# Gate and up of three row groups by seven block products for eight, statistics on ScalarE, and x added by accumulating transfers

## The chip, the cores and the metric

The kernel runs on one core of one Trainium2 chip. The metric is the device time of one execution in microseconds (us). The core has five engines that follow their own instruction lists and wait for one another through semaphores: TensorE (PE, matrix products, with PEld for its weight loads), VectorE (DVE), ScalarE (ACT), GpSimd (POOL) and SyncE (SP, which here issues transfers).

## The reference, cut to what matters

```python
xn = _layernorm(x, axis=-1)                       # x: 2048 rows of 512, float32
s = irfft2(rfft2(xn) * (w_r + 1j * w_i))          # over rows and columns
gate, up = xn @ W_gate, xn @ W_up                 # 512 -> 1376 each
g = silu((relu(gate) * up) @ W_down)              # 1376 -> 512
return x + s * g
```

## The kernel before

**Precision.** Each float32 operand of a product is split into two float16 halves, high and low, and a product is three matmuls (`PASSES`: high by high, high by low, low by high) that accumulate in float32 in PSUM. So each operand costs two extra instructions wherever it is made: a cast to the high half, on ScalarE, and a subtraction that leaves the low half, on VectorE.

**The spectral path** (left factor `s`). The rows come in eight loads of 256 (`load_x`, 0 to 7). `stats` and `deviation`/`deviations` give the layer norm, `normalise` writes `xf`, `fold` makes the sums and differences of mirrored columns (`eo`, `ee`, `xs`), `split` the halves, and `first_stage` is the first transform along the rows (`s1`, tile `t`, to the scratch `A_d` in HBM). Eight `fft_chunk` calls follow: `y_stage`, `x_stage`, the multiplication by the filter (tiles `tt`, `po`, `pf`), `z_stage`, `v_stage`, and the scratch `C_d`. `last_stage`, eight times, reads `C_d` (tile `ct`), does the last transform (`s2`), scales it on ScalarE (`zz`) and unfolds the columns (`ae`, `ye`, `sv`).

**The gated path** (right factor `g`). The rows are four groups of 512 (index `c` or `k`). The 1376 hidden columns are ten blocks of 128 and a last one of 96 (`TAIL`). `product(c, f, i)` multiplies one group by one block of the gate (i = 0) or up (i = 1) weights: 12 matmuls of 512 columns, four of the inner dimension by three passes. The rows enter transposed, as tile `xT`; `turn` makes it for groups 1 to 3 by a DMA transposition, `turn_row` for group 0 on PE. `rectify` (ScalarE) and `hidden` (VectorE, ScalarE) evaluate relu(gate)·up and its two halves, tile `h16`; `down` multiplies by the down weights (tile `dn`), `gate` applies silu, tile `g`.

**The end.** `finish(c, i)` loads a 128-row block of x again (`xt`), multiplies `sv` by `g`, adds x, and stores. The last block of group 3 is done in two halves of columns (`columns`), the second in tile `dn_3b`.

**The order.** Nothing above runs in the order of the text. Every `step` gives an engine, an estimated cost, the names that it reads and writes, and perhaps a due time; `Plan.run` places all steps on the five engines by those estimates, the due times and the number of buffers in each pool, and then emits each engine's instructions in that order. The table of numbers at the top of the file (`T0`, `LOADS`, `LOADX`, `FIRST`, `MID`, `LAST`, ...) sets the due times. PSUM is three pools of two buffers here: `gu` for gate and up, `dn` for down, and `F` for the transforms (`gu` holds one bank each, `F` two).

The first work of PE is `keep_busy`, 78 matmuls on a constant (tile `idle`), until the first weights and rows are there. InOrder.__getattr__ wraps every engine call, so the profile gives one line (L64) to nearly every instruction; rows are told apart by the tiles' names.

```python
def product(c, f, i, rows=slice(0, 4), tag="gu"):
    ...
            for k in range(4):
                for h, l in PASSES:
                    w = wgt[:, k, 2 * h, :] if f == TAIL else wgu[g][:, h, i, k, o:o + P]
                    matmul(t[:, rows], w, xT[:, rows, l * 4 + k, :], start=n == 0, stop=n == 11)
```

## Time and profile before

| | |
|---|---|
| median of 3 runs | 411.29 us (411.02 to 412.25) |
| the profiled execution | 410.83 us, of which its span, first to last instruction, is 409.1 us |
| PE busy | 402.5 us of the span |
| DVE busy | 306.6 us |
| ACT busy | 190.0 us |
| POOL busy | 47.6 us |
| moved by DMA | 51.72 MB |
| granted PE clock | 0.997 of full speed |

How to read it: "busy" is the time in which an engine executes, and an engine that is not busy waits for a name that another engine or a transfer writes. A row such as `t<-s,t 128x896 f16<-128x896 f32 x2` says: two instructions that write tile `t` from tiles `s` and `t`, 128 partitions by 896 elements. An engine runs its instructions in the order of its list, so a wait holds up all that stands behind it.

### The profile page before, as it was taken

To read this page: it belongs to the slowest core of one execution; us is meant where nothing else is said; L and a number is where in the kernel's file an instruction comes from. 1 tells how busy PE (TensorE), PEld (TensorE's weight loads), DVE (VectorE), ACT (ScalarE), POOL (GpSimd) and SP (SyncE) were. 2 spreads that over 40 slices of the span, in tenths; PEclk is the share of its full clock that TensorE was granted. 3 is DMA by queue.
4 is the path that set the end of the run, shared out by engine and by line. 5 is a ranking of instruction groups with operands and counts; after the bars stand their busy time and mean duration, and the time that the engine had idled before them with its cause. 6 is when DMAs were issued, how large, how long until landed. Compare 5 with 4: busy or idle time off the path is not lost.

```text
span 409.1 us, 7662 instructions
## 1 busy us (share of the span) xinstructions
PE 402.5 (98%) x3023; PEld 213.4 (52%) x3023; DVE 306.6 (75%) x646; ACT 190.0 (46%) x359; POOL 47.6 (12%) x68
## 2 busy tenths in 40 slices
PE   8899999999999999999999999999999999999995
PEld 7784444544444444545465455556455445444554
DVE  3959999999999993515776977878863325999973
ACT  5999655435452549320445434536432327223321
POOL 0000000000000000001230312311311006133320
PEclk9999999999999999999999999999999999999998
DMA  8970210317138269753005144142322089656511
GB/s 285 416 253 6 98 49 3 92 64 154 44 111 145 59 182 355 209 170 116 2 0 168 34 135 125 58 155 57 115 51 53 0 192 221 210 177 211 176 53 52
DMA packets 34948, 51.72 MB, mean 126 GB/s; under 512 B 15392, under 2 KB 17024, under 8 KB 34912
## 3 DMA queue, kind: packets, MB, share of 16 engines
q1 hardware_dynamic: 34624, 50.71, 41.4%
q10 hardware_dynamic: 288, 0.52, 0.5%
q8 instruction: 23, 0.38, 0.4%
q14 instruction: 13, 0.11, 0.1%
HBM read 35.48 MB, written 12.60 MB: 118 GB/s over the span
## 4 chain that ended last, share of the span: by engine, by line
PE 98%; DVE 0%; ACT 0%; issue 0%
PE gu L64 55%; PE dn L64 27%; PE s L64 3%; PE z L64 3%; PE xx L64 3%; PE idle L64 2%; PE y L64 2%; PE v L64 2%; PE dn_3b L64 1%; PE head L64 0%; ACT xT L64 0%; PE sum L64 0%; DVE xT L64 0%; ACT g L64 0%; DVE sv L64 0%
## 5 line engine op out<-in xcount | busy, mean ns | idle before, releaser
L64 PE MATMUL gu<-xT,wgu 128*128 128x512 f16 (+1 forms) x1032 | 214.8, 364 | 1.2 <-ACT xT L64 1.0
L64 PEld LDWEIGHTS <-wgu 128*128 128x128 f16 x1032 | 99.4, 98 | 105.0 <-issue 4.6
L64 PE MATMUL dn<-wds,h 128*128 128x512 f16 (+2 forms) x528 | 115.5, 373 | 0.0
L64 PEld LDWEIGHTS <-h 128*128 128x128 f16 (+1 forms) x561 | 53.7, 98 | 57.7 <-issue 1.8
L64 DVE TENSOR_TENSOR h<-gu,r 128x512 f32<-128x512 f32 (+2 forms) x52 | 33.6, 646 | 26.4 <-PE gu L64 24.5
L64 ACT ACTIVATE h<-h 128x512 f16<-128x512 f32 (+1 forms) x44 | 27.4, 626 | 52.4 <-DVE h L64 50.6
L64 POOL TENSOR_TENSOR po<-tt,tt 128x256 f32<-128x256 f32 x16 | 14.8, 924 | 282.3 <-DVE tt L64 243.2
L64 ACT ACTIVATE r<-gu 128x512 f32<-128x512 f32 (+1 forms) x44 | 26.1, 593 | 30.3 <-PE gu L64 30.0
L64 DVE TENSOR_TENSOR h<-h,h 128x512 f16<-128x512 f32 (+1 forms) x44 | 29.9, 696 | 6.9 <-ACT h L64 6.8
L64 POOL TENSOR_TENSOR ae<-zz 128x128 f32<-128x128 f32 (+1 forms) x32 | 21.3, 698 | 62.5 <-ACT zz L64 43.2
L64 DVE SCALAR_TENSOR_TENSOR tt<-xsp,cw,wt 128x512 f32<-128x512 f32 x32 | 25.6, 863 | 0.0
L64 ACT ACTIVATE g<-dn,cdi 128x512 f32<-128x512 f32 (+1 forms) x16 | 10.3, 673 | 25.9 <-PE dn L64 25.8
L64 DVE TENSOR_TENSOR z<-z,z 128x1024 f16<-128x1024 f32 x8 | 9.8, 1222 | 14.1 <-ACT z L64 14.1
L64 DVE TENSOR_TENSOR sv<-sv,g 128x512 f32<-128x512 f32 (+1 forms) x17 | 11.8, 722 | 7.5 <-ACT g L64 6.9
L64 PE MATMUL gu<-xT,wgt 128*64 128x256 f16 (+1 forms) x144 | 16.9, 309 | 0.0
L64 DVE SCALAR_TENSOR_TENSOR wgu<-raw,p,wgu 128x512 f16<-128x512 f32 x20 | 14.3, 746 | 0.3 <-ACT wgu L64 0.3
L64 ACT ACTIVATE wgu<-raw 128x512 f16<-128x512 f32 x20 | 12.3, 619 | 4.0 <-DMA raw<-in_w 4.0
L64 DVE BATCH_NORM_STATS2 st<-x 128x6 f32<-128x512 f32 x16 | 10.8, 676 | 4.4 <-DMA x<-in_x 4.4
L64 ACT ACTIVATE xs<-xs 128x1024 f16<-128x1024 f32 x8 | 8.4, 1054 | 11.7 <-DVE xs L64 11.7
L64 PEld LDWEIGHTS <-wgt 128*64 128x64 f16 (+1 forms) x144 | 9.6, 106 | 7.4 <-issue 1.7
L64 DVE TENSOR_TENSOR xt<-xt,sv 128x512 f32<-128x512 f32 (+1 forms) x17 | 11.6, 710 | 2.5 <-DMA xt<-in_x 2.3
L64 DVE TENSOR_TENSOR a<-y,a 128x1024 f16<-128x1024 f32 x8 | 9.7, 1217 | 4.9 <-ACT a L64 4.9
(135 smaller groups left out, 431.8 us busy)
## 6 DMA issues: line engine op xcount, KB each, us to landing
A_d<-t SPq DMA_DIRECT2D x16, 256.0 KB, 3.3
rw<-in_wl SPq DMA_DIRECT2D x8, 512.0 KB, 8.7
wt<-in_wl SPq DMA_DIRECT2D x8, 512.0 KB, 4.9
at<-A_d SPq DMA_DIRECT2D x8, 512.0 KB, 5.3
C_d<-t SPq DMA_DIRECT2D x16, 256.0 KB, 3.3
ct<-C_d SPq DMA_DIRECT2D x16, 256.0 KB, 5.9
xt<-in_x SPq DMA_DIRECT2D x16, 256.0 KB, 3.0
out<-xt SPq DMA_DIRECT2D x15, 256.0 KB, 2.1
```

Source lines behind the costliest of these rows:

```text
L64: return lambda *args, **kw: self.tc.keep_in_program_order(f(*args, **kw))
```

## The change

- **Gate and up of groups 1 to 3 by Strassen's scheme.** For a pair of hidden blocks (`FAST`, five pairs; the last block stays as it was) the rows of a group are cut in two halves, the inner dimension in two halves, and gate and up are the two column blocks. Seven block products (p = 1 to 7, `fast_product`) take the place of eight. One product is 12 matmuls of 256 columns: two hidden blocks by two of the inner dimension by three passes. They accumulate in three PSUM tiles, `faa`, `fab` and `fad`, that are copied out and added as they grow (`fast_rest`): per pair and group three copies and two casts on ScalarE, and on VectorE three tensor additions or subtractions and four combined operations.
- **The operands of those products.** `weight_sums` loads the raw gate and up weights of each block again (`again`), scales them on ScalarE, forms four sums and differences (`t_0` to `t_9`), and splits them into `wt` and over the first half of the up weights in `wgu`. `prepare` reads the normalised rows back from a new scratch `X_d` (written by `keep_x`), splits and transposes them to `xT` as `turn` did, and does the same with four sums and differences of row halves, tiles `sf`, `s`, `S`.
- **Statistics of loads 2 to 7 on ScalarE** (two passes with an accumulated output for each block), and `normalise` there too.
- **The filter's products** in `fft_chunk`: the filter is scaled by `cw` on ScalarE first, and two VectorE instructions of 1024 elements take the place of four of 512; `common` is two instructions for four.
- **The unfolding of `ae`** goes from POOL to VectorE.
- **x is added by transfers.** Four DMAs copy x into the output early; `finish` multiplies `sv` by `g` and stores it with an accumulating DMA that POOL issues. The last block keeps the addition. `g` of groups 0 to 2 is put in a scratch `G_d` and read back.
- **Pools and numbers.** `gu` and `dn` become one pool `w` of four; `k4` has 10 buffers for 12, `k2` 8 for 10, `xg` 3 for 5; `ff_steps` no longer mixes `down` in; the table of due times is new.

```diff
+FAST = ((0, 1), (2, 3), (4, 5), (6, 7), (8, 9))
+NFAST = [0, 5, 5, 5]
+ROOM = {"k4": 10, "k2": 8, "s": 5, "h16": 5, "ht": 1, "xg": 3}
+LATE = ('ACT', 'ACT')
+UNFOLD, MIX = "DVE", "POOL"
-LOADS, LOADX, LOADU = [8.09, 4.17, 5.72, None, None, None, None], [7.68, 3.63], -2.46
+LOADS, LOADX, LOADU = [19.5, -7.9, 0.83, None, None, None, None], [15.63, 9.9], 1.38
-NORM, TURN1 = (('ACT', 'ACT'), ('ACT', 'DVE')), 'PE'
+NORM, TURN1 = (('DVE', 'ACT'), ('DVE', 'DVE')), 'PE'
...
     def stats(c, q, j):
...
+            for i in range(2):
+                step("ACT", act(512) + .2, lambda i=i: ACT.activation(to(i), of(i), AF.Copy, accum_out=mv()[:, 0, i:i + 1]),
+                     reads=x_names(c, i), writes=[(f"mv{c}", 0, i), (f"xf{c}", i)])
...
+    def keep_x(c):
+        step("SP", .6, lambda: SP.dma_start(X_d[c], T[f"xf{c}"][:, :, 0:D]), reads=[(f"xf{c}", 0), (f"xf{c}", 1)], writes=[("X_d", c)], kb=512)
...
+    def fast_product(c, pair, p):
+        bank = f"fa{'abd'[{1: 0, 6: 0, 7: 0, 4: 0, 2: 1, 5: 2, 3: 2}[p]]}{c}_{pair[0]}"
...
+            for fi, f in enumerate(pair):
+                n = 0
+                for k in range(2):
+                    for h, l in PASSES:
+                        matmul(T[bank][:, fi], W(f, k, h), X(k, l), start=p in (1, 2, 5) and fi == n == 0, stop=fi == 1 and n == 5, skip_group_check=p in (6, 7, 4, 3))
+                        n += 1
...
+    def fast_rest(c, pair, p):
+        a, b, d = (f"fa{k}{c}_{pair[0]}" for k in "abd")
...
+        if p in (1, 6, 7):
+            k = {1: 0, 6: 1, 7: 2}[p]
+            tile_of(s[k], "s", [P, D], F32)
+            step("ACT", act(512), lambda: ACT.activation(T[s[k]], flat(a), AF.Copy, scale=2.0 ** -22 if k else 1.0), reads=[a], writes=[s[k]], due=due - 1.5)
+        if p == 2:
+            step("DVE", dve(512), lambda: DVE.tensor_add(T[s[0]], flat(b), T[s[0]]), reads=[b], writes=[s[0]], due=due)
+        if p in (7, 3):
...
+            step("DVE", stt(512), lambda: DVE.scalar_tensor_tensor(T[s[k]], flat(d), 2.0 ** -22, T[s[k]], op0=ALU.mult, op1=ALU.add),
...
+        if p == 4:
+            step("DVE", stt(512), lambda: DVE.scalar_tensor_tensor(T[s[2]], flat(a), 0.0, T[s[2]], op0=ALU.max, op1=ALU.mult), reads=[a], writes=[s[2]], due=due)
...
-    def ff_steps(c, lag=6):
-        for f in range(NFT):
...
+        if pairs:
+            fast(0, 1, 2, 6, 5, 7)
+            for n in range(1, len(pairs)):
+                fast(n, 1)
+                fast(n - 1, 4, 3)
+                fast(n, 2, 6, 5, 7)
...
-        put("POOL", "tensor_add", lambda: ac()[:, :, 0:64], lambda: a0()[:, :, 0:64], a2, 128, [zn], (aen, 0))
+        put(UNFOLD, "tensor_add", lambda: ac()[:, :, 0:64], lambda: a0()[:, :, 0:64], a2, 128, [zn], (aen, 0))
...
+            if not plain:
+                step("POOL", 1.2, lambda t=t, cols=cols: POOL.dma_start(out[:, 2 * c + i, cols], t(), accum_op=ALU.add), reads=[(n, part), ("out", c // 2)], due=due, lag=3.5)
+                continue
...
+    for k in range(NBL):
+        n = 4 * k + 4 - (k == NBL - 1)
+        step("SP", .6, lambda k=k, n=n: SP.dma_start(out[:, 4 * k:n], x[:, 4 * k:n]), writes=[("out", k)], kb=2048, lead=1, due=COPIES[0] + COPIES[1] * k)
```

Three places in the lists of instructions, before and after. First, SP's first transfers; the names are `cS` a small constant, `x` the first rows, `raw` the raw gate and up weights. Before:

```order
L64 DMA cS<-in_c_s 128x135
L64 DMA x_120<-in_x 128x512 x2
L64 DMA raw_0_131<-in_w 128x512
L64 DMA raw_1_139<-in_w 128x512
L64 DMA x_144<-in_x 128x1024
```

And after:

```order
L73 DMA cS<-in_c_s 128x135
L73 DMA raw_0_139<-in_w 128x512
L73 DMA raw_1_146<-in_w 128x512
L73 DMA x_151<-in_x 128x512 x2
L73 DMA raw_0_163<-in_w 128x512
L73 DMA raw_1_171<-in_w 128x512
L73 DMA x_177<-in_x 128x1024
```

The first rows have moved behind two weight blocks, and the second load of rows behind four.

Second, VectorE in the products of group 1. Before, with `h_1_1` a hidden block of the group, `xs` and `xf` parts of a later load's folding:

```order
L64 TENSOR_TENSOR xs_1398<-ee_1382 128x2x64 x2
L64 TENSOR_TENSOR xs_1398<-ee_1382 128x2x63
L64 TENSOR_SCALAR xf_1407<-x_1135,mv_1276,q_1295 128x512 x2
L64 TENSOR_TENSOR h_1_1_1427<-gu_1_1_1385,r_1_1400 128x512
L64 TENSOR_TENSOR xs_4_1409<-xs_1398,xs_4_1409 128x2x512
```

And after, where `s_1_0` and `s_1_2` are partial results of its first and second pair, `t_3` and `t_4` weight sums, and `t_2<-s_2` a low half of a first transform:

```order
L73 TENSOR_TENSOR wgu_81<-t_3_1365,wgu_81 128x2x128
L73 TENSOR_TENSOR wt_3_103<-t_3_1365,wt_3_103 128x768
L73 SCALAR_TENSOR_TENSOR s_1_0_1418<-fad_0_1333,s_1_0_1418 128x512
L73 TENSOR_TENSOR s_1_2_1400<-fab_2_1403,s_1_2_1400 128x512
L73 TENSOR_TENSOR t_4_1465<-again_1349 128x512
L73 TENSOR_TENSOR t_2_1463<-s_2_1421,t_2_1463 128x2x448
L73 SCALAR_TENSOR_TENSOR s_1_0_1418<-faa_0_1290,s_1_0_1418 128x512
L73 SCALAR_TENSOR_TENSOR s_1_0_1384<-fad_0_1333,s_1_0_1384 128x512
```

Between the operations that free a product tile there stand weight sums now, beside the transforms of later loads.

Third, VectorE around its last gate and up block of group 3 (`h_3_10`). Before, six of the eight `last_stage` calls stand ahead of it, and these are its neighbours:

```order
L64 TENSOR_TENSOR h_3_9_4613<-h_3_9_4600,h_3_9_4613 128x512
L64 TENSOR_TENSOR h_3_10_4702<-gu_10_1_4616,r_10_4610 64x256 x2
L64 TENSOR_TENSOR h_3_10_4702<-gu_10_0_4578,r_10_4610 32x512
L64 TENSOR_TENSOR ye_4687<-ae_4684,zz_4673 128x2x128 x2
L64 TENSOR_TENSOR h_3_10_4720<-h_3_10_4702,h_3_10_4720 96x512
```

And after:

```order
L73 SCALAR_TENSOR_TENSOR s_3_8_4915<-s_3_8_4838,s_3_8_4915 128x512
L73 TENSOR_TENSOR h_3_10_5073<-gu_10_1_4991,r_10_4968 64x256 x2
L73 TENSOR_TENSOR h_3_10_5073<-gu_10_0_4932,r_10_4968 32x512
L73 TENSOR_TENSOR ae_5094<-zz_5079 128x2x64 x2
L73 TENSOR_TENSOR ae_5094<-zz_5079 128x2x63 x2
L73 TENSOR_TENSOR ae_5127<-zz_5092 128x2x64
L73 TENSOR_TENSOR ye_5129<-ae_5094,zz_5079 128x2x128 x2
```

All eight `last_stage` calls, with the unfolding of `ae`, have moved behind the last product of group 3; on PE all of `s2` and all of `down` of group 3 stand behind it too.

Of the kernel before, what the change touches and what calls it, by code (L numbers as in the profile page):

```python
# [26 lines left out]

TAIL_COLS = ((0, 0, 96, 0, 256), (1, 64, 96, 96, 352), (1, 0, 64, 128, 192))
# [4 lines left out]
T0, DOWN, FIRST, FIRST_STEP, MID, MID_STEP, LAST, LAST_STEP = 5.52, 50.66, 44.31, 17.14, 179.63, 14.68, 274.73, 15.17  # L33
LOADS, LOADX, LOADU = [8.09, 4.17, 5.72, None, None, None, None], [7.68, 3.63], -2.46
FOLDS, FOLD_LEAD, MARGIN = ['DVE', 'DVE', 'DVE', 'DVE', 'DVE', 'DVE', 'DVE', 'DVE'], 14.21, 1.83
# [4 lines left out]
HURRY, SLOW, SLOW_TO = -2.62, 1, 14.66  # L40
# [190 lines left out]
def kernel(ctx: ExitStack, tc: tile.TileContext, x, w_in, wd, wd_tail, wl, ew, sp, c_r, c_d, c_m, c_x, c_s, out):  # L231
# [14 lines left out]
    E_d = dram.tile([2, 2, 1024], F32, name="E_d")  # L246

# [15 lines left out]
    sc = cpool.tile([P, NFT], F32, name="scd")  # L263
    mw = cpool.tile([P, NCH + 3], F32, name="mw")
# [7 lines left out]
    T = Plan({"k4": 12, "k2": 10, "h16": NFT, "xg": NBL + 1, "F": 2, "gu": 2, "dn": 2, "q": 4, "q4": 2, "mv": 4, "m": 4, "p": 4, "am": 1, "mid": 3})  # L272
    step = T.step

    def tile_of(name, tag, shape, dtype, padded=None):
        pools = {"F": psum, "gu": psum, "dn": psum}
        T.tile(name, tag, lambda: pools.get(tag, bpool).tile(shape, dtype, name=name, tag=tag, bufs=T.room[tag]))
# [24 lines left out]
    def stats(c, q, j):  # L302

        def run(i):
            st = T[f"st{c}"][:, 6 * i:6 * i + 6]
            DVE.bn_stats(st, T[f"x{c}"][:, i, :])
            DVE.bn_aggr(T[f"mv{c}"][:, i, :], st)
        tile_of(f"st{c}", "q", [P, 12], F32)
# [27 lines left out]
    def deviations(cs):  # L336
# [3 lines left out]
        tile_of(name, "q4", [P, 3, 4], F32)  # L340

        def run():
            w, y, t = (T[name][:, i, :] for i in range(3))
            b = T[name].bitcast(I32)
            for j, c in enumerate(cs):
                DVE.tensor_scalar(w[:, 2 * j:2 * j + 2], T[f"mv{c}"][:, :, 1], EPS, 64.0 / XS ** 2, op0=ALU.add, op1=ALU.mult)
# [5 lines left out]
        step("DVE", 2.4, run, reads=[(f"mv{c}", i) for c in cs for i in range(2)], writes=[(name, 2)], port=True)  # L352

    def normalise(c, q, at, engines=("DVE", "DVE")):

        tile_of(f"xf{c}", "k4", [P, 2, D + 2], F32)

        def run(i):
            to, x = T[f"xf{c}"][:, i, 0:D], T[f"x{c}"][:, i, :]
            if engines[i] == "ACT":  # L360
                ACT.activation(to, x, AF.Identity, bias=T[q][:, 0, i:i + 1], scale=at()[:, i:i + 1])
# [7 lines left out]
    def turn(c, lows):  # L369

        tile_of(f"x16_{c}", "k4", [P, 2, 2, D], F16)
        if c % 2 == 0:
            tile_of(f"xT{c // 2}", "xg", [P, 4, 8, P], F16)
        x16, xf = (lambda: T[f"x16_{c}"]), (lambda i: T[f"xf{c}"][:, i, 0:D])
        for i in range(2):
            step("ACT", act(512), lambda i=i: ACT.activation(x16()[:, i, 0, :], xf(i), AF.Copy),
                 reads=[(f"xf{c}", i)], writes=[(f"x16_{c}", i, 0)])
            e, cost = ((DVE, dve(512)), (POOL, pool(512)))[lows[i] == "POOL"]
            step(lows[i], cost, lambda i=i, e=e: e.tensor_sub(x16()[:, i, 1, :], xf(i), x16()[:, i, 0, :]),
                 reads=[(f"xf{c}", i), (f"x16_{c}", i, 0)], writes=[(f"x16_{c}", i, 1)], port=True)  # L380
# [117 lines left out]
    def group_scale(g):  # L498
        nf = len(GROUPS[g])
        tile_of(f"sum{g}", "dn" if g < 2 else "F", [P, 4], F32)  # L500
        tile_of(f"p{g}", "p", [P, 2, 4], F32)
        step("PE", .2, lambda: matmul(T[f"sum{g}"][:, :2 * nf], ones, T[f"m{g}"][:, :2 * nf], start=True, stop=True),
             reads=[(f"m{g}", j, i) for j in range(nf) for i in range(2)], writes=[f"sum{g}"])
        step("DVE", .52, lambda: scale_of(T[f"sum{g}"][:, :2 * nf], T[f"p{g}"][:, :, :2 * nf], 9), reads=[f"sum{g}"], writes=[f"p{g}"], port=True)

    def group_split(g):
        fs = GROUPS[g]
        nf = len(fs)
        for j, f in enumerate(fs):
            cols = slice(j * P, j * P + fwidth(f))  # L510
            cs = lambda i, j=j: T[f"p{g}"][:, 0, 2 * j + i:2 * j + i + 1]
# [26 lines left out]
        def rhos():  # L538
            inverse_of(T[f"p{g}"][:, :, :2 * nf])
            DVE.scalar_tensor_tensor(rho[:, fs[0]:fs[-1] + 1], T[f"p{g}"][:, 1, 0:2 * nf:2], 2.0 ** 14,  # L540
                                     T[f"p{g}"][:, 1, 1:2 * nf:2], op0=ALU.mult, op1=ALU.mult)
# [169 lines left out]

    def rectify(c, f):
# [5 lines left out]
    def hidden(c, f):  # L718
        e, n32, n16 = fwidth(f), f"h32_{c}_{f}", f"h16_{c}_{f}"
        tile_of(n32, "k2", [P, 4, P], F32)  # L720
        tile_of(n16, "h16", [P, 2, 4, P], F16)
        h32, h16, r = (lambda: T[n32]), (lambda: T[n16]), (lambda: T[f"r{c}_{f}"])
# [9 lines left out]
        step("ACT", act(512), lambda: ACT.activation(h16()[:e, 0], h32()[:e], AF.Copy), reads=[n32], writes=[(n16, 0)])  # L732
        step("DVE", dve(512), lambda: DVE.tensor_sub(h16()[:e, 1], h32()[:e], h16()[:e, 0]), reads=[n32, (n16, 0)], writes=[(n16, 1)], port=True)

    def down(c, f, rows, part=0):
        e, cols = fwidth(f), columns(c, rows[0])[part]
        names = ["dn0_23" if c == 0 and i >= 2 else f"dn{c}_{i}" + "b" * part for i in rows]
        if f == 0:
            for name in dict.fromkeys(names):
                tile_of(name, *(("F", [P, 2, D]) if name == "dn0_23" else ("gu" if part else "dn", [P, cols.stop - cols.start])), F32)  # L740

        def run():
            for i, name in zip(rows, names):
                t = T[name][:, i - 2, :] if name == "dn0_23" else T[name]
                for n, (h, l) in enumerate(PASSES):
                    matmul(t, T[f"h16_{c}_{f}"][:e, h, i, :], wds[:e, f, l, cols],
                           start=f == 0 and n == 0, stop=f == NFT - 1 and n == 2)
        cost = pe(3 * len(rows), cols.stop - cols.start)
        step("PE", cost, run, reads=[("wd", f), ("wdl", f), (f"h16_{c}_{f}", 0), (f"h16_{c}_{f}", 1)], writes=names, due=tick(cost))

    def gate(c, i, part=0):
        name, cols = "dn0_23" if c == 0 and i >= 2 else f"dn{c}_{i}" + "b" * part, columns(c, i)[part]
        if f"g{c}" not in T.tiles:
            tile_of(f"g{c}", "xg", [P, 4, D], F32)
        step("ACT", act(cols.stop - cols.start) + .1, lambda: ACT.activation(
            T[f"g{c}"][:, i, cols], T[name][:, i - 2, :] if name == "dn0_23" else T[name], AF.Silu, scale=cdi),
            reads=[name, "scd"], writes=[(f"g{c}", i, part)], due=clock[0] + 4)

    def ff_steps(c, lag=6):
        for f in range(NFT):  # L760
            product(c, f, 0)
            rectify(c, f)
            if f >= lag:
                down(c, f - lag, (0, 1))
            product(c, f, 1)
            hidden(c, f)
        e = NFT - 1
        for f, i in [(f, i) for i in range(2) for f in range(NFT - lag, e - i)] + [(e, 0), (e - 1, 1), (e, 1)]:
            down(c, f, (i,))
            if f == e:  # L770
                gate(c, i)
# [4 lines left out]
        for f, i, part in order:  # L776
            down(c, f, (i,), part)
            if f == e:
                gate(c, i, part)


    def fft_chunk(q, due):
        a16n, xsn, pfn, pon, p16n, z16n, t9n, atn, wtn = (f"{k}_{q}" for k in ("a16", "xsp", "pf", "po", "p16", "z16", "t9", "at", "wt"))
        for n, tag, shape, dtype in ((atn, "k4", [P, 2, 2, D], F16), (f"cm{q}", "k2", [P, 2, 2, 2, 64], F16),
# [6 lines left out]
                                     (t9n, "k4", [P, 2, 2, D], F16), *((f"tt{i}_{q}", "k2", [P, 16, 32], F32) for i in range(4))):  # L791
# [57 lines left out]
        if q == 0:  # L849
            tile_of("zb", "gu", [P, 2, 2], F32)  # L850
# [11 lines left out]

# [335 lines left out]
```

More of the change, by code (lines that the diff above doesn't have):

```diff
@@ L351, in run, with normalise @@
                 DVE.scalar_tensor_tensor(y, t, 3.0, y, op0=ALU.add, op1=ALU.mult)
-        step("DVE", 2.4, run, reads=[(f"mv{c}", i) for c in cs for i in range(2)], writes=[(name, 2)], port=True)
-    def normalise(c, q, at, engines=("DVE", "DVE")):
-        tile_of(f"xf{c}", "k4", [P, 2, D + 2], F32)
+            for j, c in enumerate(cs):
+                DVE.tensor_mul(T[name][:, 3, 2 * j:2 * j + 2], y[:, 2 * j:2 * j + 2], T[f"mv{c}"][:, 1])
+        step("DVE", 2.6, run, reads=[(f"mv{c}", i) for c in cs for i in range(2)], writes=[(name, 2)], port=True)
+    def normalise(c, q, at, engines=("DVE", "DVE"), bias=None):
+        if c < 2:
+            tile_of(f"xf{c}", "k4", [P, 2, D + 2], F32)
         def run(i):
@@ L656, in tick, with product @@
         t = clock[0]
-        clock[0] += cost * (SLOW if cost < 2 and t < SLOW_TO else 1.0 if t < 60 else 1.17)
+        clock[0] += cost * (SLOW if cost < 2 and t < SLOW_TO else 1.0 if t < 60 else SLOWER)
         return t
-    def product(c, f, i, rows=slice(0, 4), tag="gu"):
+    def product(c, f, i, rows=slice(0, 4), tag="w"):
         g = next(n for n, fs in enumerate(GROUPS) if f in fs)
@@ L710, in product, with h16_of, h16_tile, h16_names @@
              writes=out, due=tick(cost))
+    def h16_of(c, f):
+        return (T[f"ht{c}"] if f == TAIL else T[f"h16_{c}_{f // 2}"][:, :, f % 2])
+    def h16_tile(c, f):
+        n = f"ht{c}" if f == TAIL else f"h16_{c}_{f // 2}"
+        if n not in T.tiles:
+            tile_of(n, *(("ht", [P, 2, 4, P]) if f == TAIL else ("h16", [P, 2, 2, 4, P])), F16)
+        return n
+    def h16_names(c, f, h, rows=(0, 1)):
+        return [(h16_tile(c, f), f, h, r) for r in rows]
     def rectify(c, f):
@@ L761, in ff_steps, with fast @@
+    def ff_steps(c):
+        pairs = FAST[len(FAST) - NFAST[c]:]
+        def fast(n, *ps):
+            for p in ps:
+                fast_product(c, pairs[n], p)
+                fast_rest(c, pairs[n], p)
+        for f in range(2 * (len(FAST) - len(pairs))):
             product(c, f, 0)
             rectify(c, f)
-            if f >= lag:
-                down(c, f - lag, (0, 1))
             product(c, f, 1)
             hidden(c, f)
+        if pairs:
[4 more added lines that the diff above has]
+                fast(n, 2, 6, 5, 7)
+        product(c, TAIL, 0)
+        rectify(c, TAIL)
+        if pairs:
+            fast(len(pairs) - 1, 4, 3)
+        product(c, TAIL, 1)
+        hidden(c, TAIL)
@@ L767, in ff_steps @@
         e = NFT - 1
[L768 to L771, printed above, removed]
+        for f in range(NFT):
+            down(c, f, (0, 1))
+        for i in range(2):
+            gate(c, i)
         if c == NBL - 1:
@@ L1046 @@
             for i in range(2):
-                product(0, f, i, slice(2 * h, 2 * h + 2), ("gu", "dn", "F")[f])
+                product(0, f, i, slice(2 * h, 2 * h + 2), ("w", "w", "F")[f])
             if h:
@@ L1061 @@
             gate(0, i)
+    for n, f in enumerate([f for p in FAST[len(FAST) - max(NFAST):] for f in p]):
+        T.within(f"ts{f}", "ts")
+        weight_sums(n, f)
     for c in range(1, NBL):
+        T.within(f"pr{c}", "pr")
+        prepare(c)
+        T.within(None, None)
         ff_steps(c)
```

273 lines of the change are left out of this document (198 added, 75 removed).

## The prediction

> **What bounds the kernel now.** I read the page first: busy times, slices, and the chain that ended last.
>
> ```profile
> PE 402.5 (98%) x3023; PEld 213.4 (52%) x3023; DVE 306.6 (75%) x646; ACT 190.0 (46%) x359; POOL 47.6 (12%) x68
> PE   8899999999999999999999999999999999999995
> DVE  3959999999999993515776977878863325999973
> PEclk9999999999999999999999999999999999999998
> PE 98%; DVE 0%; ACT 0%; issue 0%
> ```
>
> PE works all the time at full granted clock and carries 98% of the chain. So a matmul taken away shortens the kernel by its own time, as long as no other engine comes to the front. The DVE slices show which: it is at nine tenths from slice 4 to 15, and again near the end. Next the chain in order of time (start, length, both in us, and what), for the pace of PE and for what stands at the end:
>
> ```profile
> 20.21 7.86 PE gu L64 x72
> ...
> 317.80 5.18 PE gu L64 x24
> ...
> 379.47 1.43 PE gu L64 x24
> 380.90 0.78 PE s L64 x24
> ...
> 402.17 2.64 PE dn_3b L64 x24
> 404.81 0.02 issue
> 404.83 0.48 ACT g L64
> ...
> 405.80 0.42 DVE xt L64
> ```
>
> The 72 are gate and up matmuls of 256 columns: 109 ns each. The 24 at 317.80 are of 512 columns: 216 ns. Both have a weight load of their own, so halving the columns costs nothing per column. The row at 379.47 is the last product of the last hidden block; it ends at 380.90. What follows on PE to 404.81 is 23.9 us. The last addition ends at 406.22 and the span at 409.1: 2.9 us for the last store. The profiled execution took 410.83, that is 1.7 beyond its span, and it lies 0.5 under the median of 411.29. About 0.3% of that median, 1.2 us, is what a measurement of this kernel can tell from no change.
>
> Then VectorE's instructions in order of time, for the spacing of one kind in a row (start, length of the run, what):
>
> ```profile
> 62.19 1.22 DVE L64 TENSOR_TENSOR xs<-xs,xs 128x1024 f16<-128x1024 f32 x1
> 65.42 1.29 DVE L64 TENSOR_TENSOR h<-h,h 128x512 f16<-128x512 f32 x2
> 14.53 1.41 DVE L64 SCALAR_TENSOR_TENSOR wgu<-raw,p,wgu 128x512 f16<-128x512 f32 x2
> 355.89 0.76 DVE L64 TENSOR_TENSOR ye<-ae,zz 128x256 f32<-128x256 f32 x2
> 40.76 0.89 DVE L64 TENSOR_TENSOR xs<-ee 128x130 f32<-128x130 f32 x4
> 352.08 1.29 DVE L64 TENSOR_TENSOR sv<-ye 128x510 f32<-128x510 f32 x2
> 342.44 1.81 DVE L64 TENSOR_TENSOR sv<-ye 128x510 f32<-128x510 f32 x2
> 385.33 1.56 DVE L64 TENSOR_TENSOR h<-gu,r 64x256 f32<-64x256 f32 x3
> ```
>
> Instructions overlap a little, so the spacing is less than the length: 0.60 us for 512 (two in 1.29, one alone 0.69), 0.665 for a combined operation of 512, 0.335 for 256, 0.20 for 128, and some 1.13 for 1024. For 768, which no row shows, I put 0.87 between its neighbours.
>
> **The change, part by part.** *Seven products for eight.* A pair of hidden blocks in a group took 48 matmuls of 512, 10.37 us; it takes 84 of 256, 9.17. Fifteen times 1.2 is 17.9 us less PE work. Nothing covers PE, so this is all on the path.
>
> *The work on VectorE.* Rows by kind (count, then busy us and mean ns):
>
> ```profile
> L64 DVE SCALAR_TENSOR_TENSOR tt<-xsp,cw,wt 128x512 f32<-128x512 f32 x32 | 25.6, 863 | 0.0
> L64 DVE TENSOR_TENSOR pf<-po 128x128 f32<-128x128 f32 x32 | 12.3, 443 | 0.0
> L64 DVE BATCH_NORM_STATS2 st<-x 128x6 f32<-128x512 f32 x16 | 10.8, 676 | 4.4 <-DMA x<-in_x 4.4
> L64 DVE TENSOR_SCALAR xf<-x,mv,q 128x512 f32<-128x512 f32 x13 | 6.6, 543 | 0.0
> L64 POOL TENSOR_TENSOR ae<-zz 128x128 f32<-128x128 f32 x16 | 10.7, 692 | 62.5 <-ACT zz L64 43.2 <-DVE ye L64 19.3
> L64 ACT ACTIVATE h<-h 128x512 f16<-128x512 f32 x40 | 24.9, 626 | 47.2 <-DVE h L64 45.5 <-PE dn L64 1.7
> ```
>
> Added: per pair and group 3 x 0.60 + 4 x 0.665 for 4 x 0.60, 2.06 more, times 15 is 30.9; weight sums of ten blocks at 0.60 + 3 x 0.335 + 0.87, 24.8; the sums of rows, three times 4 x 0.60 + 2 x 1.13, 14.0; `ae`, 32 at 0.20, 6.4. Taken away: 12 of 16 statistics 8.1 and their small ones some 1.2; 12 of 13 normalisations 6.1; `tt` from 25.6 to 16 x 1.13, 7.5; `pf` from 12.3 to 16 x 0.335, 6.9; fifteen additions of x at 0.60, 9.0. Net +37, so VectorE goes from 306.6 to about 344 us, in a kernel that is to be shorter. ScalarE gains some 116 instructions of the 0.62 class (statistics, raw weights, filter, partial results), +72 to about 260; that is two thirds, and I give it no term of its own. POOL loses 21.7 of `ae` and gets fifteen issues.
>
> What matters is where VectorE's work lies. I counted its instructions in the new order, stage by stage, at these spacings, against PE's. While PE does group 1's products (44.9 us: 30 products of 1.31, two `s`, the last block), VectorE has 49.6 (28 of 256, 20 of 512, 16 combined, 8 of 768, five larger, the rest small). From there to the last product of group 3, PE has 202 and VectorE 167. Behind that product PE has 34.8 and VectorE 39.8. So VectorE is the longer in two places.
>
> *The start.* The first rows go behind two weight blocks on SP. Engine rows:
>
> ```profile
> 6.32 0.69 DVE L64 BATCH_NORM_STATS2 st<-x 128x6 f32<-128x512 f32 x1 [0.41 <-DMA x<-in_x]
> 7.67 0.63 ACT L64 ACTIVATE wgu<-raw 128x512 f16<-128x512 f32 x1 [1.27 <-DMA raw<-in_w]
> 13.35 1.03 PE L64 MATMUL gu<-xT,wgu 128*128 128x256 f16 x8 [0.96 <-ACT xT L64]
> ```
>
> The second block of rows was awaited until 6.32, the first weight block behind them until 7.67. In exchanged places the rows come 1.4 to about 2.5 later, with statistics, normalisation, transposition and the first product at 13.35 all behind them; the second load is behind four blocks. From 0 (if the transfers share the engines evenly) to +4; I take +2.3. `keep_busy` covers nothing here; it only fills.
>
> *Group 1.* VectorE is 4.7 us longer, and a product can begin only when one of the four `w` tiles is free, which a late VectorE instruction delays. The same stage first waits for transposed operands; landing times of transfers (issue to landing, us, last column):
>
> ```profile
> xT<-x SPq DMA_TRANSPOSE x6, 4.5
> ct<-C_d SPq DMA_DIRECT2D x16, 256.0 KB, 5.9
> C_d<-t SPq DMA_DIRECT2D x16, 256.0 KB, 3.3
> out<-xt SPq DMA_DIRECT2D x15, 256.0 KB, 2.1
> ```
>
> The four transpositions of group 1 stand on SP behind the read of `X_d` and the stores of `g`, which wait for ScalarE and for `down` of group 0; product 5, third in line, needs the third of them, 4.5 us after VectorE made it. `down` of group 0 (21 us) hides the load itself. Bounds 0, since four tiles are some three products of slack, to 8, the 4.7 and about three on entering. I take +2, nearer to zero because `down` of group 1 (29 us) lets VectorE catch up before group 2. `prepare` of groups 2 and 3 lies in stages where VectorE has slack; cost nothing, and if that cover were gone, each is 8 us of VectorE.
>
> *The end.* Behind the last product now stand eight `s2` at 0.78 (6.2), all of `down` of group 3 (99 matmuls of 512, 66 of 256: 28.6): 34.8 for 23.9, so the last product comes 10.9 earlier for that. It ends at 380.9 - 17.9 - 10.9 + 2.3 + 2 = 356.4. VectorE then has 32 `ae` (6.4), 32 `ye` (10.7), 16 `sv` (9.6), 15 products with g (9.0), four of 256 (1.3), the last hidden block (1.6) and two low halves (1.2): 39.8. POOL's elementwise work is gone there, so I use 1.29 for two `sv`, not the 1.81 that stands beside POOL's `ae`. It waits first for `zz` of ScalarE, and `s2` for `ct`: the last `v` lies 13 us of PE ahead of the first `s2`, the store and the load take 3.3 + 5.9 and two evictions 2, and the loads share SP; +2 (0 to 5). VectorE is done at 398.2. PE alone would allow 356.4 + 34.8 + 0.5 for the last silu and 3.3 for six operations, 395.0, so VectorE ends last.
>
> *The last transfers.* They are POOL's, accumulating; no row shows one. The nearest are the plain store of 2.1 (with what follows it 2.9 to the end of the span) and, for three that become ready within 2 us, three of them in series, 6.3. Nothing speaks for a gain. I take 4.0, nearer to the single store, with 2.9 to 8 kept. By the Trainium skill, "DMA: Bandwidth & Descriptors", section on the anatomy of one DMA on the gpsimd path, a transfer issued there takes 2.0 us plus its bytes at 436 GB/s, an estimate of 2.6 for 256 KB; by it the sum would be 1.4 lower. No row here shows it.
>
> The sum: 398.2 + 4.0 = 402.2 of span, and 1.7 beyond it: **404 us**. So of 17.9 us taken from PE some 7 remain: the start takes 2.3, group 1 2, and the rest is the end, where VectorE outlasts PE.
>
> **The rivals.** *PE stays the bound.* VectorE runs as it did from slice 4 to 15, at 95% without holding PE up, and is not later than PE at the end: 380.9 - 17.9 - 10.9 + 2.3 + 34.8 + 0.5 + 3.3 + 2.9 + 1.7 = 398 us. For it speaks that those slices cost PE nothing; against it the 39.8 for 34.8.
>
> *VectorE falls behind in group 1 and PE waits for all of it:* +8 instead of +2, 410 us, and more if weight sums come late for the next pair. For it: it is the only stage where VectorE has more than PE over 45 us. Against: the catching up after it.
>
> *The accumulating transfers go one at a time and outlast everything.* The first is ready about 12.6 us behind the last product, and fifteen follow one another. At the 3.3 of a store such as `C_d<-t` each, the last lands at 356.4 + 12.6 + 49.5, and the run takes 420 us, slower than before. It decides from 2.7 us each, where the sum is the median of before. The row for it is 342.44 against 352.08: VectorE beside POOL takes 0.5 more for two `sv`, so the two hold each other up. Against it: plain stores overlap, 2.1 each. The Trainium skill, "SBUF — State Buffer", section "SBUF: two separate sides", calls the port that DVE and GpSimd share an exclusive lock, held by a VectorE operation with two SBUF inputs only against a GpSimd operation that reads SBUF, and says that descriptors are starved by VectorE's two-port modes. The rows at 342.44 and 352.08 agree with a lock; by that rule `ye` and `sv` would not starve the fifteen issues, and this rival would not come.
>
> **How the numbers follow.** The forecast, 399 to 409 by the bounds of its terms, 0.53. PE the bound, 398, 0.15. Behind in group 1, 410 to 414, 0.19, of which 0.04 is faster, 0.08 the same, 0.07 slower. Transfers one at a time, from 412 up, 0.13. Faster 0.53 + 0.15 + 0.04 = 0.72, the same 0.08, slower 0.20. The range 395 to 413 leaves out the transfers' case and a little below.
>
> **What would show it.** PE: 84 matmuls of 256 per pair at 109 ns, about 385 us busy. The first `gu` near 15.6. VectorE near 344 us and its share at nine tenths in group 1 and at the end; the chain there through VectorE, not PE. Waits of PE for `fa` tiles or `S` in group 1 of a few us. The last `gu` ending near 356, then some 40 us of `ae`, `ye`, `sv`, `xt`. The forecast is wrong if PE waits over 8 us in group 1, if POOL's transfers land more than 8 us after VectorE's last instruction, or if the 256-column products run slower than 109 ns.

## The result, and the profile after

The changed kernel takes 435.77 us in the median (433.65 to 436.85) beside 411.77 for the kernel before: a ratio of 1.058, 95% interval 1.053 to 1.062. It is slower by 24 us; 404 was forecast. The profiled execution took 436.08, its span is 434.3. For `act_turns`, `pool_loads` and `best2`, below, executions over 1.5% above the fastest of the same kernel, at a lower granted clock, are left out of the times. First the busy times, two rows of slices and the chain's shares:

```profile
PE 393.1 (91%) x3563; PEld 269.6 (62%) x3563; DVE 339.2 (78%) x715; ACT 257.8 (59%) x488; POOL 43.8 (10%) x51
PE   9799999999799999995999999994999999998440
PEclk9899999999999999999899999997999999999685
PE 33%; DMA 10%; DVE 5%; issue 5%; ACT 4%; POOL 2%; SPq 1%; POOLq 0%; DVEq 0%; ACTq 0%
```

PE has 9.4 us less work than before, and VectorE and ScalarE are nearly as busy as forecast (344 and 260). But PE is idle for 41 us of the span, where before it was 7, and the chain now passes through transfers. The slices, counted from 0, show where: a little in 1 and 10, much in 18 and 27, most in the last three. PE's waits by what ended them (total us, times, longest):

```profile
PE dn L73 <- DVE h L73: 6.9, 1, 6.9
PE faa L73 <- ACT s L73: 6.0, 3, 3.9
PE y L73 <- DMA cm<-in_c_m: 5.6, 1, 5.6
```

The chain at these places (start, length, what):

```profile
196.39 6.89 DMA xT<-x
203.39 1.09 ACT t L73 x2
...
206.05 2.70 PE faa L73 x12
...
210.49 1.31 PE faa L73 x12
...
298.03 3.83 DMA cm<-in_c_m
302.00 1.47 PE y L73 x48
...
370.70 7.43 DMA ct<-C_d
378.15 9.29 DMA gt<-G_d
...
398.36 5.77 DMA out<-xt
...
426.47 0.89 POOLq L1403
```

Three stories stand in these rows. At 203.39 ScalarE writes `t` when a transposition of rows has landed (`t` and the tile that the transposition reads come from one pool of ten buffers, `k4`), and PE goes on at 206.05. At 302.00 PE has waited for `cm`, which SP issued only at 298.03. From 370 on the chain runs from `ct` to the reads of g (`gt`) to the accumulating transfers. SP's own rows say why `cm` was late (start, time to issue, what):

```profile
177.23 1.40 SPq L73 DMA_TRANSPOSE xT<-x  x1
...
186.00 4.51 SPq L73 DMA_TRANSPOSE S<-s  x1
...
283.33 4.58 SPq L73 DMA_TRANSPOSE xT<-x  x1
...
289.34 4.50 SPq L73 DMA_TRANSPOSE S<-s  x1
...
294.95 2.01 SPq L73 DMA_TRANSPOSE S<-s  x1
297.08 0.90 SPq L73 DMA_DIRECT2D at<-A_d  x1
298.03 0.47 SPq L73 DMA_DIRECT2D cm<-in_c_m  x1
```

Between 283 and 299 us a plain transfer is issued in 0.4 to 0.9 us; a transposition holds the queue for 1.4 to 4.6 in these rows. There are twelve instead of six, and those of groups 2 and 3 now stand among the loads of the filter and of the second transform. The landing times, and the end on PE and VectorE:

```profile
out<-xt POOLq DMA_DIRECT2D x15, 256.0 KB, 5.1
gt<-G_d SPq DMA_DIRECT2D x12, 256.0 KB, 4.7
xT<-x SPq DMA_TRANSPOSE x6, 6.7
S<-s SPq DMA_TRANSPOSE x6, 5.6
```

```profile
370.77 1.50 PE L73 MATMUL gu<-xT,wgt 128*64 128x256 f16 x24
...
425.55 0.75 DVE L73 TENSOR_TENSOR xt<-xt,sv 128x256 f32<-128x256 f32 x2
```

The last product ends at 372.3 (forecast 356.4), VectorE 54 us later (41.8), the span another 8 us later (4.0).

The waits cost more than their length. In windows of the span (length, busy PE, PEld, DVE, ACT, POOL, then the granted clock, the busy share of the 16 transfer engines, and what they moved in GB/s):

```profile
185.00:210.00 25.00, 20.46 (x159) 14.34 (x158) 16.03 (x41) 16.95 (x31) 0.00 (x0) 0.93 1.05 252
278.00:305.00 27.00, 21.27 (x256) 12.63 (x253) 17.52 (x22) 12.35 (x18) 6.21 (x8) 0.88 0.91 211
```

Behind the wait of 3.9 us the first product took 2.70 us, the one at 210.49 again 1.31. The Trainium skill, "TensorE: Matmul & The Clock Gate", Part 1, says that PE's clock is halved after an idle window of some 3.4 us. The rows agree: half pace stands behind the waits of 3.9, 5.6 and 6.9 us, and behind the two of group 1, 0.5 and 1.5 us, there is none. In the runs below a wait of 3.6 us left the granted clock at 1.00 (`plain_stores`, at 403.7), and one of 3.8 us was followed by a clock of 0.50 (`early_gt`, at 207.1).

A fourth such place is the start, where no single wait is that long. PE runs out of `keep_busy` at 11.9 us and has 1.1 us of work up to 15.7, between waits of 1.5 and 1.2; then the granted clock is 0.58 of full speed where it was 1.00 before the change. From 15 to 19 us, PE alone, the kernel before and the changed one:

```profile
15.00:19.00 4.00, 4.00 (x40) 1.00 0.99 401
15.00:19.00 4.00, 3.31 (x19) 0.58 1.04 384
```

### The profile page after: what moved, and what is told of

Read it like the earlier page. It is cut to its first block, busy times and chain, and to the rows that moved or that the text cites. A ratio compares the mean times of both kernels' runs of the same rounds, so it can differ in the third digit from the quotient of the medians.

```text
span 434.3 us, 9003 instructions
## 1 busy us (share of the span) xinstructions
PE 393.1 (91%) x3563; PEld 269.6 (62%) x3563; DVE 339.2 (78%) x715; ACT 257.8 (59%) x488; POOL 43.8 (10%) x51
## 4 chain that ended last, share of the span: by engine, by line
PE 33%; DMA 10%; DVE 5%; issue 5%; ACT 4%; POOL 2%; SPq 1%; POOLq 0%; DVEq 0%; ACTq 0%
PE faa L73 11%; PE fad L73 6%; PE dn L73 4%; DMA gt<-G_d 3%; DMA xT<-x 3%; PE z L73 3%; PE fab L73 2%; PE xx L73 2%; ACT xf L73 2%; DMA ct<-C_d 2%; POOL out L73 2%; PE y L73 2%; PE gu L73 2%; PE v L73 2%; DMA out<-xt 1%
## 5 line engine op out<-in xcount | busy, mean ns | idle before, releaser
L73 PE MATMUL dn<-wds,h 128*128 128x512 f16 (+1 forms) x480 | 107.2, 377 | 6.9 <-DVE h L73 6.9
L73 PEld LDWEIGHTS <-h 128*128 128x128 f16 x510 | 48.7, 99 | 60.4 <-DVE h L73 7.4
L73 PEld LDWEIGHTS <-wt 128*128 128x128 f16 x540 | 52.7, 99 | 16.0 <-issue 6.1
L73 PE MATMUL gu<-xT,wgu 128*128 128x512 f16 (+1 forms) x312 | 54.6, 336 | 1.9 <-ACT xT L73 1.2
L73 PE MATMUL faa<-S,wt 128*128 128x256 f16 x360 | 44.2, 273 | 2.7 <-ACT s L73 2.0
L73 PE MATMUL fad<-S,wgu 128*128 128x256 f16 x360 | 44.7, 274 | 0.0
L73 ACT ACTIVATE s<-faa 128x512 f32<-128x512 f32 x45 | 26.4, 592 | 17.3 <-PE faa L73 15.6
L73 PE MATMUL faa<-xT,wt 128*128 128x256 f16 x180 | 23.4, 282 | 4.0 <-ACT s L73 3.9
L73 PE MATMUL fab<-xT,wgu 128*128 128x256 f16 x180 | 22.1, 273 | 0.0
L73 PE MATMUL faa<-xT,wgu 128*128 128x256 f16 x180 | 22.1, 272 | 0.0
L73 POOL DMA_DIRECT2D out<-xt x15 | 13.3, 975 | 66.2 <-DVE ye L73 40.5
```

The source lines that it names most:

```text
L73: return lambda *args, **kw: self.tc.keep_in_program_order(f(*args, **kw))
```

## Experiments

"Before" was run beside every kernel and took 411.2 to 411.7 us. Where an edit keeps every engine's order, it changes only what a step issues, not the plan.

**Transpositions as copies (`copy_turns`).**

```diff
-SP.dma_start_transpose(T[f"xT{k}"][...], T[n]...)
-SP.dma_start_transpose(T[f"S{k}"][:, half], T[s16]...)
+SP.dma_start(T[f"xT{k}"][...], T[n]...)
+SP.dma_start(T[f"S{k}"][:, half], T[s16]...)
```

> All twelve DMA transpositions of groups 1 to 3 (six of rows, six of row sums) are plain copies of the same tiles; the products then work on untransposed numbers. Every engine's list keeps its order. Theory (a transposition holds SP's queue for up to 4.8 us, and the loads of `cm`, `at` and `rw` queued behind it come late): the waits of PE of 3.9 us at 202 and 5.6 us at 296 go, and with them some 3 us of matmuls at half pace behind them: 422 to 428 us. Rival (VectorE and ScalarE are behind there by their own work): the waits stay, 432 to 437 us.

422.45 us (421.23 to 424.38), 13.3 less. Both waits are gone, and so are the two of group 1, whose four transpositions are copies too: the last block of group 1 begins at 148.0 instead of 150.3. The last product ends at 357.0 instead of 372.3. SP's rows for the third group's last three:

```profile
273.54 0.92 SPq L73 DMA_DIRECT2D xT<-x  x1
...
276.82 1.46 SPq L73 DMA_DIRECT2D S<-s  x1
...
279.51 0.97 SPq L73 DMA_DIRECT2D S<-s  x1
```

They take 6.9 us from the start of the first to the end of the last, against 13.6 from 283.33 to 296.96 above.

The transfer engines differ as well. First the changed kernel's packets, then those of `copy_turns`, and then the windows of `copy_turns`, which is 2 to 10 us ahead in them, for the two above:

```profile
DMA packets 60059, 72.80 MB, mean 168 GB/s; under 512 B 28592, under 2 KB 37392, under 8 KB 59632
DMA packets 36827, 72.79 MB, mean 174 GB/s; under 512 B 3824, under 2 KB 12624, under 8 KB 36400
```

```profile
185.00:210.00 25.00, 24.74 (x237) 19.16 (x235) 19.59 (x43) 21.11 (x39) 0.00 (x0) 1.00 0.99 353
278.00:305.00 27.00, 27.00 (x318) 18.86 (x317) 22.57 (x31) 15.81 (x23) 11.32 (x12) 1.00 0.55 183
```

For the same bytes, twelve transpositions make 24768 more packets under 512 B, and with them the 16 engines are busy for 1.05 and 0.91 of the windows at 252 and 211 GB/s. With copies they move 353 GB/s in the first, at 0.99, and in the second they are busy for 0.55. So a transposition may have three prices: its queue, its source buffer, and time of the engines that move all transfers.

**The added six alone (`copy_s`).** Only the second line of that edit.

> Only the six transpositions of row sums, which the change adds, are plain copies; the six of rows, which it moves later, stay. Theory (every transposition on SP counts the same): about half of the 13.3 us that all twelve cost, 427 to 431 us, one of PE's two waits smaller and the other still there. Rival (the moved ones alone are late): 433 us and above; or (the added ones alone): 422 to 424 us.

428.55 us (423.81 to 429.26), 7.2 less: about half; one run of the four lies 4.6 us under the other three. The wait for `cm` is 2.3 us instead of 5.6.

**Plain stores (`plain_stores`).**

```diff
-POOL.dma_start(out[:, 2 * c + i, cols], t(), accum_op=ALU.add)
+POOL.dma_start(out[:, 2 * c + i, cols], t())
```

> The fifteen transfers that POOL issues store without accumulating, so x is missing from the output; every engine's list keeps its order. Theory (an accumulating transfer takes long to land, 5.1 us in the median, and holds one of the buffers of `xt`): VectorE's waits of 6.1 us for those transfers go, PE's wait of 7.0 us at 400 shrinks, the 8 us behind VectorE's last instruction become about 4: 422 to 428 us. Rival (what costs is that POOL issues them, or VectorE's own work): 433 to 437 us, landing times as before.

426.89 us (426.28 to 427.98), 8.9 less. The transfers, and VectorE's last instruction in a span of 424.5:

```profile
out<-xt POOLq DMA_DIRECT2D x15, 256.0 KB, 2.7
```

```profile
419.55 0.76 DVE L73 TENSOR_TENSOR xt<-xt,sv 128x256 f32<-128x256 f32 x2
```

2.7 us instead of 5.1, 4.2 us behind VectorE's end instead of 8.0, and PE waits 3.6 us for its hidden block instead of 6.9. So the price is the accumulation, not that POOL issues: the plain stores are POOL's too.

**Reads of g ahead (`early_gt`).**

```diff
+for j in range(3): SP.dma_start(T[f"gt0_{j}"], G_d[0, j])   # ahead of the first ct
```

> The first three reads of `g` (`gt`) are issued ahead of the sixteen loads `ct` instead of behind them; nothing else moves. Theory (the first `gt` waits behind 4 MB of `ct` in the transfers): VectorE's wait of 5.8 us at 381 goes, and 3 to 6 us of the time with it: 430 to 433 us. Rival (the later transfers take the time back, or PE's wait for a hidden block behind them is what counts): 434 to 437 us.

431.15 us (429.87 to 432.53), 4.6 less. VectorE's first product with g has no wait now:

```profile
383.86 0.68 DVE L73 TENSOR_TENSOR xt<-sv,gt 128x512 f32<-128x512 f32 x1
```

PE's wait at 400 fell to 0.6 us: the hidden block stood behind that product in VectorE's list.

**All three (`three`).**

> All three edits together: plain copies for the transpositions, plain stores for the accumulating ones, three reads of g ahead of `ct`. Theory (three separate costs, 13.3 + 8.9 + 4.6 = 26.8 us): 408 to 413 us. Rival (the plain stores and the early reads remove the same wait of PE at the end): 413 to 418 us.

409.70 us (405.93 to 411.57, nine runs), ratio to before 0.995 (0.992 to 0.998): 26.1 less than the changed kernel, against a sum of 26.8. The three costs are separate. `three` leaves out the transposition and the x of the output, so it measures and cannot replace the kernel; the same holds for `three_pool` and `no_fast_three`. Its busy times, last product and last VectorE instruction:

```profile
PE 388.8 (95%) x3563; PEld 267.5 (66%) x3563; DVE 339.7 (83%) x715; ACT 258.0 (63%) x488; POOL 38.1 (9%) x51
```

```profile
357.87 1.50 PE L73 MATMUL gu<-xT,wgt 128*64 128x256 f16 x24
...
402.92 0.75 DVE L73 TENSOR_TENSOR xt<-xt,sv 128x256 f32<-128x256 f32 x2
```

**Without the seven products (`no_fast`, `no_fast_three`).** `NFAST = [0, 0, 0, 0]`, in the second together with the three edits.

> No group uses the seven products: gate and up as before the change, no weight sums, no row sums; statistics on ScalarE, the scratch of rows and of g, the accumulating transfers and the new numbers stay. The plan's order changes with it. Theory (most of the loss is at the end and in the queue of SP, not in the seven products): PE has some 14 us more work and fewer waits, the end keeps its price: 418 to 430 us. Rival (the seven products, their weight sums and row sums are the loss): 408 to 414 us.

> The three edits together, and no group uses the seven products; the plan's order changes with it. What the seven products are worth where nothing else stands in the way is its time less 409.7 us. Theory (PE bounds the kernel up to the last product, so its 14 to 18 us come through, less what VectorE's weight sums and row sums take): 420 to 428 us. Rival (the 37 us of VectorE work that they add eat the gain at the end): 409 to 415 us.

441.27 us (440.34 to 442.66) and 431.03 (430.36 to 432.73). So the seven products were worth 5.5 us in the kernel as changed and 21.3 where nothing stands in their way. Both kernels have a plan whose due times were set for the seven products, and PE waits for hidden blocks there (8.8 and 7.2 us in the first), so the two differences are rough; their sign is not. `no_fast` was expected below the changed kernel by both theories; both were wrong on it. PE's work in it:

```profile
PE 408.8 (93%) x3023; PEld 215.6 (49%) x3023; DVE 281.0 (64%) x602; ACT 222.9 (51%) x427; POOL 43.6 (10%) x51
```

15.7 us more than with the seven products, for a forecast of 17.9; both kernels have matmuls at half pace behind long waits, so this difference is rough too.

**x added by VectorE again (`added_x`).** `plain = True` for all sixteen blocks, without the copies of x into the output.

> The end as before the change: x is loaded and added by VectorE, the stores are SP's; no copies of x into the output, no accumulating transfers; the seven products and the rest stay. The plan's order changes with it. Theory (the accumulating transfers cost 8.9 us and save VectorE 9 us at an end where it is the longer engine): 428 to 437 us. Rival (the accumulating transfers are worth nothing at all to VectorE): 424 to 428 us.

435.70 us (434.41 to 438.19): no difference. VectorE has 348.3 us of work instead of 339.2. In this plan the accumulating transfers cost as much as the loads, additions and stores that they replace.

**The unfolding on POOL (`three_pool`).**

> The kernel with the three edits together (409.7 us), and the 32 additions of `ae` of the last stage run on POOL, idle there, instead of VectorE; the lists are otherwise in the same order. Theory (with the transfers out of the way VectorE's 40 us of work bounds the end): 6.4 us less for VectorE, 4 to 6 us of them in the time, 404 to 406 us. Rival (POOL takes 0.69 us for each where VectorE takes 0.20, and the results come later): 409 to 415 us.

413.45 us (412.41 to 415.15), 3.7 more than `three`. VectorE's last instruction moved from 403.7 to 407.5: taking 32 additions off the engine that ends last made the end later.

**Which queue (`act_turns`, `act_loads`, `pool_loads`).** In the first the transpositions are on ScalarE's queue, in the others 24 loads on ScalarE's or on POOL's.

```diff
-SP.dma_start_transpose(...)            # act_turns, twelve
+ACT.dma_start_transpose(...)
-SP.dma_start(T[f"rw{q}"] ... T[f"cm{q}"] ... T[wtn] ...)   # act_loads; pool_loads with POOL
+ACT.dma_start(...)
```

> The twelve transpositions are issued from ScalarE's queue instead of SP's, at the same places of the plan; everything else keeps its order and the computation is whole. Theory (a transposition is held up by the loads that are under way on the same queue: 1.4 us where SP had issued nothing for 4 us, 4.2 to 5.4 behind loads of 512 KB; ScalarE's queue has no loads): the loads behind are no longer late, ScalarE loses 1 to 2 us at each of twelve places where it has slack: 423 to 429 us. Rival (a transposition holds whichever queue issues it for its 4.5 us): ScalarE is held up 4.5 us twelve times, and PE with it: 432 to 445 us.

> The loads of the filter (`rw`, `wt`) and of `cm`, 24 in all, are issued from ScalarE's queue instead of SP's, at the same places of the plan; the transpositions stay on SP and the computation is whole. Theory (the loads are late because they stand behind transpositions in one queue): PE's wait for `cm` at 296 and most of that at 202 go, 424 to 430 us. Rival (while a transposition is under way loads of any queue are slow, or ScalarE's own order holds the loads up): PE waits as long or longer, 433 to 445 us.

> The 24 loads `rw`, `wt` and `cm` are issued from POOL's queue, which has little else to do there, instead of SP's; the transpositions stay on SP and the computation is whole. Theory (a load is late because it stands behind a transposition in its queue): PE's wait for `cm` near 296 and VectorE's and ScalarE's waits for `rw` go, 424 to 430 us. Rival (what holds the engines up is the buffer that a transposition reads, which the next tile must wait for until it has landed): the waits turn into waits for the transpositions themselves, 433 to 440 us.

454.70 us (452.92 and 456.47), 440.39 (438.91 to 441.40), 440.21 (438.39 to 442.26): none gained. On ScalarE's queue (ACTq) one transposition held it, and with it ScalarE, for 9.5 us (`act_turns`). With the loads there and the transpositions on SP, ScalarE waits for a transposition to land (`act_loads`):

```profile
299.82 9.52 ACTq L73 DMA_TRANSPOSE S<-s  x1
```

```profile
298.50 0.60 ACT L73 ACTIVATE xsp<-xx 128x512 f32<-128x512 f32 x1 [7.29 <-DMA xT<-x]
```

With the loads on POOL's queue the transpositions on SP are as long as ever, and what stays there is late (PE's wait in `pool_loads`):

```profile
283.47 5.92 SPq L73 DMA_TRANSPOSE xT<-x  x1
```

```profile
PE y L73 <- DMA at<-A_d: 4.2, 1, 4.2
```

So the theory that the lateness of the three kinds of load on SP's queue is the whole cost falls. PE's wait for `cm` is gone in `act_loads` and `pool_loads`, and others stand in its place, of engines that wait for a transposition to land as ScalarE does at 298.50. The Trainium skill, "DMA: Bandwidth & Descriptors", section "Issuing engines are not separate DMA queues", says that transfers run on the same 16 engines whoever starts them, and that a second issuing engine saves only the issuing. These three runs agree in that none gained; they do not tell apart what is due to busy transfer engines and what to buffers.

**Transpositions ahead of their neighbours (`turns_first`).** In this kernel what the plan puts on SP within 4 us ahead of a transposition is issued behind it.

> The loads and stores that the plan puts on SP within 4 us ahead of a transposition are issued behind it instead; the transpositions stay on SP, everything else keeps its order, and the computation is whole. Theory (a transposition's issue lasts until the transfers under way at its start have landed): most of the transpositions now take 1.4 to 2.5 us instead of 4 to 5, the four of a group take about 11 us in a row instead of 17, and 4 to 9 us go: 427 to 432 us. Rival (a transposition holds the queue for its own sake, whatever went before it): still 4 to 5 us each, and what was moved behind it is later: 435 to 442 us.

446.46 us (445.35 to 447.70), 10.7 more. SP's rows and PE's longest wait:

```profile
193.59 1.63 SPq L73 DMA_TRANSPOSE S<-s  x1
...
197.55 4.36 SPq L73 DMA_TRANSPOSE S<-s  x1
...
293.00 1.95 SPq L73 DMA_TRANSPOSE xT<-x  x1
```

```profile
PE faa L73 <- ACT s L73: 12.4, 3, 6.1
```

The theory was right on some times to issue and wrong on the kernel's. The one at 193.59, with nothing issued for 5.9 us, takes 1.6 us, and the one at 293.00, with only a load of 2 KB in the 4 us before, 2.0; the one at 197.55, behind a load of 512 KB at 196.43 and a store, takes 4.4. But SP now stands still from 187.7 to 193.6, until the row sums are ready, and the loads wait behind it.

**Whole kernels from the parts (`gt_in_place`, `best`, `best2`, `best3`).** `gt_in_place` is `early_gt` with the product with g written over `sv` and accumulated from there; `best3` is `turns_first` with `gt_in_place`.

> Three reads of g ahead of `ct` (431.2 us alone), and the product with g is written over `sv` and accumulated from there, so that it takes no buffer of `xt`. Theory (VectorE's waits of 6 us for the accumulating transfers are waits for that buffer): 424 to 428 us. Rival (the buffers of `sv` are then held as long, and the last transfer counts): 429 to 433 us.

> A whole kernel: the seven products, x loaded and added by VectorE with SP's stores (435.7 us alone), three reads of g ahead of `ct`, `ae` on POOL, and the 24 loads on ScalarE's queue. If each edit is worth what it is alone (-4.6 for the reads, -4 to -6 for `ae`, -6 to -11 for the loads): 415 to 421 us, still above the kernel before. Rival (loads on ScalarE's queue hold it up, and POOL's `ae` is late): 430 us and more.

> A whole kernel: `gt_in_place` with the 24 loads on POOL's queue. If both theories hold, 414 to 421 us; by the rival for the loads, 428 to 435 us. Above the kernel before in either case.

> The same, with the three reads of g ahead of `ct` and the product with g accumulated from `sv` (429.3 us together without the moved transpositions). Theory: 419 to 425 us. Rival: 429 to 436 us.

429.25 us (428.46 to 430.63), one run of `best` at 431.62 with three from 438.33 to 445.80 (too scattered for a verdict), 433.5 (432.08 and 434.85), 439.57 (436.99 to 441.12). `gt_in_place` is 1.9 better than `early_gt`, as its rival had it: without a buffer of `xt` little is gained, but those of `sv` are held instead, so what the buffers cost is not shown. The transfers land in 6.2 us, and the span ends 9.3 us behind VectorE:

```profile
out<-sv POOLq DMA_DIRECT2D x15, 256.0 KB, 6.2
```

No whole kernel came near the kernel before.

## Why the prediction was wrong, step by step

- **Seven products for eight, -17.9 us of PE.** Right: where no long wait stands ahead, a product of 12 matmuls takes 1.31 us in the chain, 109 ns each as forecast. Before and after show 9.4 less, because the matmuls behind the long waits ran at half pace; `three`, without those of groups 2 and 3 and of the end, has 388.8 us of PE work, 13.7 under the kernel before, and still has the half pace at the start.
- **The start, +2.3.** Right on the first product of group 0, which begins at 15.69 (forecast 15.6), and short of what follows: PE then ran at a granted clock of 0.58 up to 19 us, and the last gate and up block of group 0 begins 3.2 us later than before (72.2 for 69.1). `keep_busy` was said to cover nothing here; when the rows came later it ended too soon, at 11.9 us. No run lengthened it.
- **Group 1, +2.** Right in size: PE waits 0.5 and 1.5 us there. They go when the transpositions are copies, so they were the transpositions' and not VectorE's 4.7 us, and the rival of a VectorE that falls behind did not come.
- **"`prepare` of groups 2 and 3 lies in stages where VectorE has slack; cost nothing."** This is the step that failed most. The cover named was VectorE's, and the price was that of the transpositions, in SP's queue, in the buffers of what they read and in the transfer engines. All twelve cost 13.3 us, of which the six added make 7.2. Some 2 of the 13.3 lie in group 1, where a term stood for them; some 11 lie in groups 2 and 3, where there was none. The row for it was on hand (4.5 us from issue to landing), and it was used for group 1 alone.
- **The reads of g** had no term: 4.6 us, since the first stood behind 4 MB of `ct`.
- **The last transfers, +4.0.** Mis-sized: taken near the plain store's 2.1 us, they land in 5.1, and cost 8.9 in all. The rival had them one at a time, 3.3 each; they overlapped, and its 420 us was passed for other reasons as well.
- **The estimate of 2.6 us for a transfer issued by POOL**, worked out from the Trainium skill, "DMA: Bandwidth & Descriptors", section on the anatomy of one DMA, fits the plain store of `plain_stores` (2.7) and not the accumulating one (5.1). The rule on the shared port (the Trainium skill, "SBUF — State Buffer", section "SBUF: two separate sides"), by which the end would have no trouble from VectorE, has no run that tells it apart: the plain stores beside the same VectorE work were quick, and `three_pool`, with elementwise work on both engines, was 3.7 us slower.
- **VectorE behind the last product, 41.8 us.** 44.3 in `three`, 54 in the changed kernel with its waits.

With the three costs away, `three` took 409.7: the last product ends 3.0 us later than forecast, VectorE needs 2.5 more behind it, and 0.3 lie in the last transfers and beyond the span. With these 5.8 and the 26.1, 404 becomes 436. That the last product is so near is in part luck, and more so the 357.0 of `copy_turns`: these kernels have no waits in group 1, for which the forecast held 2 us, and lose elsewhere what it did not hold. In `three` the start costs 3.7 for 2.3, and short waits of PE between 106 and 300 us some 2.3; the rest, about 1.3, stays open. PE did not bound the changed kernel, and VectorE did so only at the end.

Open: how much of the 13.3 us is the time that a transposition holds its queue, how much the time until its source buffer is free, and how much the transfer engines' time for small packets. Copies shorten all three, and no run changed one and held the others. No kernel was tried in which the transposed tiles have buffers of their own.

## What to carry to other kernels

Count a transposition by transfer as a stretch of its queue, of its source buffer, and of the engines that every other transfer needs, and look at the queue where it will stand, not only at the engine that feeds it. Work taken from the bounding engine comes through only if no wait of a few us takes its place: here the matmuls behind each such wait ran at half pace for a while, and at the start they did so behind two shorter waits with little work between them. Before a transfer's kind is changed, look for a row of that kind; where there is none, do not take the nearest row for it: the plain store of 2.1 us stood for a transfer of 5.1.

## What had not been expected of the hardware

In these runs a transposition of 512 KB took 1.4 to 2.0 us to issue wherever SP had issued nothing for over 4 us, 1.3 to 9.6 nearer behind other transfers (the longest in `best`, which has loads on ScalarE's queue), and 1.7 to 9.5 on ScalarE's queue beside SP's transfers. Twelve of them made 24768 more packets under 512 B than copies of the same tiles. An accumulating transfer of 256 KB landed in 4.7 to 7.1 us in a run's median (`no_fast`, `best2`), a plain one of the same queue in 2.7 to 3.2 (`plain_stores`, `no_fast_three`).
